# A weight word's masked bits and exponent in one PSUM bank, two banks for attention's small products, and a new slot table

## The chip, the cores and the metric

The kernel runs on one core of a Trainium2 chip. The metric is the device time of one execution in microseconds (us); three runs of the kernel before gave 510.4, 511.69 and 512.15 us, a median of 511.69.

## The reference, cut to what matters

Three layers run one after another: clustered attention, a dense layer with a rational activation, and a soft mixture of experts.

```python
q_assign = argmax(einsum('bhsd,hcd->bhsc', q_n, c_n))      # nearest of 16 centroids
k_assign = argmax(einsum('bhsd,hcd->bhsc', k_n, c_n))
scores = where(q_assign == k_assign, scale * q @ k.T, -1e9)  # 2 batches, 8 heads, 768 x 768
x = softmax(scores) @ v                                     # -> 1536 tokens x 512
h = x @ w_in                                                # 512 x 2048, given as float64
g = (a0 + a1*h + a2*h*h + a3*h**3) / (1 + |b0|*|h| + |b1|*h*h + 1e-6)
x = g @ w_out                                               # 2048 x 512, given as float64
logits = x @ phi; d = softmax(logits, 0); c = softmax(logits, 1)
out = c @ experts(d.T @ x)                                  # 8 experts, 4 slots each
```

The weights `w_in` and `w_out` come as 64-bit floats. The kernel makes 32-bit values of them itself, from the two 32-bit words of each.

## The kernel before, in words

Attention is a list of 96 units (8 pairs of heads, 12 blocks each) that one loop takes through slots n = -2 to 101 (lines 744 to 796). The order on each engine is the order in which this loop emits instructions; nothing is reordered. In slot n PE turns unit n's exponentials around (`turn`, L486, six transposes), multiplies the scores of unit n+2 (`a1_mm`, L460 and L458, four matmuls into a two-bank tile), runs the slot's small products, and some value products (`a2_av`, L499; how many is the digit of `AV`). VectorE runs the slot's small steps and then `a1_neg` of unit n+2 (L471): it reads the scores, writes them negated to SBUF and takes their minimum. ScalarE takes the exponential of unit n+1 (L475), copies unit n's turned block (L492) and runs its small steps. The score tile is a single one; unit 1's scores alone lie in the tile of the turned blocks (line 452).

The small steps are laid out by hand: `SLOT` (line 114) gives the slot of each step, and `RANK` (line 168) its engine group and its place in the slot. The groups are L and S (DMAs on SyncE), D (VectorE), G (GpSimd), A (ScalarE), P and T (PE, ahead of and behind the value products). Some steps prepare the next pair of heads (scores against the centroids, one-hot masks, high and low parts of q and k); some end a group of rows (over, wide, rows, wider, split); and some decode weights.

Decoding (`decode_steps`, line 607) takes 32 pieces of 128 x 512 weights, one SBUF tile of raw words each. `ex` masks the exponent bits of the high word, `mh` its mantissa bits, both from SBUF to SBUF on VectorE (L617). `expo` (ScalarE, L626) shifts and rebases the exponent in place. `mant` (VectorE, L629) adds the low word, scaled, to the masked bits, in place; `sign` (VectorE, L633) puts the sign on the exponent, in place. `value` (GpSimd, L638) multiplies the two. Further steps split or transpose and store the result.

All small products of PE (centroid scores L364, their transposes L374, masks L401, row factors L520, weight transposes L670, products with phi L679, L691) take a bank of the PSUM pool `psM`, three banks (line 104). A bank comes free when the reader of that product, on VectorE or ScalarE, is done. Pair 1's centroid scores are computed at the very start, right after the first scores.

Of the kernel before, what the change touches and what calls it, by code (L numbers as in the profile page):

```python
# [52 lines left out]
def tile_kernel(ctx, tc, qk, v, cenT, cenP, consts, constsb, ab, w_in, w_out, phi, w1, w2, out, dbg=None):  # L53
# [50 lines left out]
    psM = actx.enter_context(tc.tile_pool(name="psM", bufs=3, space=PSUM))  # L104
# [12 lines left out]
        scT=(0, 11, 17, 28, 40, 53, 67),
        best=(1, 12, 18, 29, 42, 55, 68),
        equal=(1, 13, 19, 29, 44, 55, 69),
        rank=(2, 13, 22, 30, 44, 55, 70),  # L120
        least=(3, 14, 23, 31, 45, 56, 70),
        alone=(4, 15, 23, 31, 47, 57, 71),
        turn=(4, 16, 24, 32, 47, 59, 73),
        masks=(5, 17, 26, 34, 48, 61, 74),
        high=(1, 9, 21, 34, 44, 57, 69),
        klow0=(1, 9, 21, 34, 46, 57, 71),
        klow1=(1, 14, 22, 39, 46, 58, 71),
        qlow0=(5, 10, 23, 38, 46, 60, 71),
        qlow1=(6, 15, 26, 38, 50, 62, 71),
        own0=(2, 10, 27, 40, 53, 67, 72),  # L130
        own1=(2, 18, 30, 38, 51, 62, 73),
        cross0=(7, 17, 30, 41, 55, 65, 80),
        cross1=(7, 17, 31, 39, 54, 65, 74),
        low0=(3, 19, 32, 40, 47, 64, 78),
        low1=(3, 15, 28, 41, 55, 64, 77),
        mask0=(6, 19, 32, 42, 53, 66, 78),
        mask1=(6, 20, 31, 42, 55, 66, 78),
        over=(7, 13, 19, 26, 32, 37, 44, 49, 56, 62, 67, 74, 81, 86, 91, 98),
# [16 lines left out]
        value=(3, 7, 8, 11, 14, 16, 20, 21, 25, 26, 29, 34, 37, 38, 40, 43, 45, 48, 50, 55, 56, 59, 63, 66, 68, 72,
               74, 76, 80, 81, 85, 88),
        store=(6, 8, 14, 14, 22, 20, 27, 25, 30, 34, 35, 36, 38, 40, 46, 45, 51, 50, 57, 56, 64, 60, 69, 71, 74,
               74, 82, 78, 87, 83, 91, 90),
        hpart=(4, 8, 18, 23, 28, 30, 37, 40, 48, 52, 61, 66, 72, 74, 83, 88),
# [1278 lines left out]
```

## Time and profile before

| | |
|---|---|
| median of three runs | 511.69 us (510.4 to 512.15) |
| the profiled execution | 510.94 us, span 509.1 us, granted clock 0.995 |
| PE busy | 495.1 us, 97% of the span |
| VectorE (DVE) busy | 403.3 us, 79% |
| ScalarE (ACT) busy | 369.5 us, 73% |
| GpSimd (POOL) busy | 272.7 us, 54% |

A row of a timeline begins with the start and the duration in us, then engine, line, operation, the output and inputs by the program's names, and in square brackets the idle time before it with what ended it. A row by line gives how many instructions there are, and the shortest, the median and the longest in ns. PE's matmuls are pipelined and their ends are modelled, so a gap of PE is drawn somewhat too short. Attention lies between about 15 and 265 us, and the dense layer and the experts behind it.

### The profile page before, as it was taken

Reading aid. Unit: us, or ns where it says so; the run is one execution under the profiler, and the core shown is the slowest. Engines: PE = TensorE matmul, PEld = TensorE weight load, DVE = VectorE, ACT = ScalarE, POOL = GpSimd, SP = SyncE. Lnnn points to the kernel's source line nnn. Section 1 sums busy time; section 2 is a strip of 40 time slices with the busy share of each in tenths; the row PEclk is TensorE's granted clock in tenths of the full one; section 3 lists DMA queues with packets and bytes.
Section 4 is the critical chain, followed back from the end, with each engine's and each line's share of the span. In section 5 each row is a group of like instructions: output and inputs, shape, how many; then the busy total and the mean of one; then the engine's idle time right before and its main releaser. Section 6 shows DMA issues by size and latency. Waiting matters only on the chain.

```text
span 509.1 us, 9715 instructions
## 1 busy us (share of the span) xinstructions
PE 495.1 (97%) x3452; PEld 336.6 (66%) x3454; DVE 403.3 (79%) x748; ACT 369.5 (73%) x653; POOL 272.7 (54%) x305
## 2 busy tenths in 40 slices
PE   7999999999999999899999999999999999999995
PEld 2667576766767566666666877776777767764363
DVE  5797989999998978978643999999799996985022
ACT  5788888888879798797863988888588776871111
POOL 2556497677683876754425755565456544651000
PEclk8999999999999999999999999999999999999999
DMA  7979798898979699882222777675567765799998
GB/s 226 255 218 267 246 271 265 241 296 233 266 225 221 237 260 238 252 216 110 82 86 101 259 268 258 238 241 208 203 224 251 256 223 192 284 339 408 420 416 321
DMA packets 40671, 124.99 MB, mean 245 GB/s; under 512 B 5744, under 2 KB 6896, under 8 KB 36016
## 3 DMA queue, kind: packets, MB, share of 16 engines
q1 hardware_dynamic: 40048, 123.66, 75.5%
q10 hardware_dynamic: 576, 0.72, 0.4%
q8 instruction: 27, 0.44, 0.4%
q14 instruction: 20, 0.16, 0.1%
HBM read 89.56 MB, written 15.73 MB: 207 GB/s over the span
## 4 chain that ended last, share of the span: by engine, by line
PE 76%; DMA 11%; DVE 8%; ACT 2%; issue 1%; ACTq 0%; DVEq 0%; SPq 0%
PE sT L486 11%; PE av L499 11%; PE h L862 9%; PE h L865 9%; PE h L863 9%; DMA wt<-w 7%; PE s L460 6%; PE s L458 5%; PE gt L909 4%; DVE e L471 3%; DMA raw<-w_in 2%; PE l L921 2%; PE dg L983 1%; DMA w_in<-w 1%; DVE mh L629 1%
## 5 line engine op out<-in xcount | busy, mean ns | idle before, releaser
L475 ACT ACTIVATE e<-e,nv 128x768 f32<-128x768 f32 x96 | 90.0, 938 | 36.1 <-DVE e L471 33.8
L471 DVE TENSOR_SCALAR_CACHE_REDUCE e<-s 128x768 f32<-128x768 f32 x96 | 91.6, 954 | 30.2 <-PE s L458 26.0
L486 PEld LDWEIGHTS sT<-cst,e 128*128 128x128 f32 x576 | 61.5, 140 | 44.2 <-ACT eT L492 21.4
L486 PE MATMUL sT<-cst,e 128*128 128x128 f32 x576 | 83.4, 281 | 1.5 <-DVE e L471 0.7
L862 PE MATMUL h<-xh,w 128*128 128x512 f32 x192 | 80.6, 420 | 0.0
L492 ACT COPY eT<-sT 128x768 f32<-128x768 f32 x96 | 75.3, 784 | 4.9 <-PE sT L486 4.6
L863 PE MATMUL h<-xl,w 128*128 128x512 f32 x192 | 75.2, 392 | 0.0
L499 PE MATMUL av<-eT,vt 128*64 128x384 f32 x384 | 75.1, 501 | 0.0
L460 PE MATMUL s<-op 128*128 128x384 f32 x192 | 72.9, 381 | 2.2 <-DVE e L471 1.8
L879 POOL TENSOR_SCALAR q<-u,babs 128x512 f32<-128x512 f32 x47 | 36.4, 775 | 68.8 <-ACT u L877 68.8
L638 POOL TENSOR_TENSOR w<-mh,ex 128x516 f32<-128x516 f32 x32 | 42.1, 1314 | 47.3 <-DVE ex L633 34.9
L458 PE MATMUL s<-op 80*128 80x384 f32 x192 | 64.7, 338 | 0.2 <-ACT op L296 0.2
L881 POOL TENSOR_TENSOR q<-q,u 128x512 f32<-128x512 f32 x47 | 61.0, 1298 | 3.9
L865 PE MATMUL h<-xh,w 128*128 128x512 f32 x192 | 52.9, 396 | 0.0
L877 ACT ACTIVATE u<-h 128x512 f32<-128x512 f32 x47 | 27.9, 594 | 29.0 <-PE h L865 29.0
L862 PEld LDWEIGHTS h<-xh,w 128*128 128x128 f32 x192 | 36.1, 188 | 16.3 <-DVE p L894 5.0
L880 DVE TENSOR_TENSOR p<-p,h 128x512 f32<-128x512 f32 x47 | 32.1, 683 | 15.6 <-ACT p L878 15.5
L865 PEld LDWEIGHTS h<-xh,w 128*128 128x128 f32 x192 | 36.0, 188 | 8.6
L863 PEld LDWEIGHTS h<-xl,w 128*128 128x128 f32 x192 | 36.2, 189 | 6.7 <-issue 0.5
L499 PEld LDWEIGHTS av<-eT,vt 128*64 128x64 f32 x384 | 22.6, 135 | 26.2 <-issue 24.7
L460 PEld LDWEIGHTS s<-op 128*128 128x128 f32 x192 | 36.2, 189 | 4.6 <-DVE e L471 3.8
L887 ACT ACTIVATE r<-q,epsc 128x512 f32<-128x512 f32 x47 | 32.8, 697 | 8.2 <-POOL q L881 6.7
(203 smaller groups left out, 938.3 us busy)
## 6 DMA issues: line engine op xcount, KB each, us to landing
wt<-w SPq DMA_DIRECT2D x32, 1024.0 KB, 7.0
w<-w_in SPq DMA_DIRECT2D x96, 256.0 KB, 3.1
op<-split SPq DMA_DIRECT2D x42, 384.0 KB, 7.1
raw<-w_in SPq DMA_DIRECT2D x16, 512.0 KB, 6.1
raw<-w_out SPq DMA_DIRECT2D x16, 512.0 KB, 5.9
w_in<-w SPq DMA_DIRECT2D x16, 512.0 KB, 5.8
raw<-qk SPq DMA_DIRECT2D x7, 768.0 KB, 7.3
w_out<-w SPq DMA_DIRECT2D x16, 256.0 KB, 4.3
```

The costliest lines, as they stand in the source:

```text
L458: PE.matmul(ps[:, c, 0:HS], o["q2"][rows, it], o["k2"][rows, w], start=False, stop=True)
L460: PE.matmul(ps[:, c, 0:HS], o["q1"][:, it], o["k1"][:, w], start=True, stop=False)
L471: DVE.tensor_scalar(e, s1s.pop(u)[:, :, 0:HS], -(D ** -0.5), None, ALU.mult, ALU.min, accum_out=nvs[g][:, rest:rest + 1])
L475: ACT.activation(es[u], es[u], AF.Exp, scale=-1.0, bias=nvs[g][:, rest:rest + 1], accum_out=sums[g][:, rest:rest + 1])
L486: PE.transpose(ps[:, j // 3, j % 3 * 128:(j % 3 + 1) * 128], e[:, j, :], ident)
L492: ACT.copy(dst, eTp.pop(u)[:, :, 0:HS].rearrange("p c (j t) -> p c j t", j=3))
L499: PE.matmul(av[g][64 * h:64 * h + 64, 0:HS], vs[g // 2][:, h, j, :], eTs[g][:, h, j, :], start=(j == 0), stop=(j == 5))
L638: POOL.tensor_tensor(w.rearrange("p (r n) -> p r n", r=3), hold["mh"].bitcast(F32), hold["ex"].bitcast(F32), ALU.mult)
L862: PE.matmul(h, wh[:, c, :], xh[t][:, c, :], start=(c == 0), stop=False)
L863: PE.matmul(h, wh[:, c, :], xl[t][:, c, :], start=False, stop=False)
L865: PE.matmul(h, wl[:, c, :], xh[t][:, c, :], start=False, stop=(c == NCC - 1))
L881: POOL.tensor_tensor(q, q, u, ALU.mult)
```

## The change

The raw tile becomes 4 x 128 words in place of 3 x 172, so that all operations take 512 elements and no pad has to be cleared. A pool `psD` of one PSUM bank is new, and `psM` has two banks in place of three. `mh` writes the masked mantissa bits to the bank of `psD`; `mant` reads them there, with the low word from SBUF, and writes to an SBUF tile of its own. After that `expo` reads the exponent bits in SBUF and writes the exponent to the same bank; `sign` reads it there, with the high word from SBUF, and writes to the SBUF tile of `ex`. `value` reads SBUF as before. Pair 1's centroid scores take the bank of `psD` too. `SLOT` and the digits of `AV` are new throughout; of the table the diff below keeps the lines of the decode steps (the first few pieces) and of a few more, and `RANK` stays.

```diff
-    psM = actx.enter_context(tc.tile_pool(name="psM", bufs=3, space=PSUM))
+    psM = actx.enter_context(tc.tile_pool(name="psM", bufs=2, space=PSUM))
+    psD = actx.enter_context(tc.tile_pool(name="psD", bufs=1, space=PSUM))
...
-        scaled=(-1, 10, 16, 27, 39, 51, 65),
+        scaled=(-1, 10, 15, 30, 40, 53, 65),
...
-        ex=(0, 2, 5, 9, 11, 14, 15, 17, 22, 23, 26, 30, 33, 36, 38, 40, 41, 44, 49, 50, 54, 57, 58, 61, 64, 67, 70,
+        ex=(-1, 4, 5, 9, 12, 14, 18, 21, 23, 27, 29, 31, 33, 36, 39, 41, 45, 47, 48, 51, 52, 55, 61, 62, 64, 67,
...
-        mh=(-1, 5, 7, 9, 11, 13, 16, 17, 21, 25, 27, 29, 32, 35, 38, 39, 42, 44, 48, 49, 52, 57, 59, 60, 65, 69,
+        mh=(-1, 3, 6, 8, 11, 15, 17, 20, 23, 25, 28, 31, 33, 35, 38, 41, 44, 46, 49, 51, 53, 58, 60, 62, 65, 67,
...
-        expo=(1, 2, 6, 9, 12, 14, 15, 17, 22, 24, 28, 31, 33, 36, 38, 41, 44, 45, 49, 52, 55, 58, 61, 62, 66, 68,
+        expo=(1, 5, 7, 10, 13, 16, 18, 21, 24, 27, 29, 32, 34, 36, 39, 42, 45, 48, 50, 52, 54, 59, 61, 63, 66, 68,
...
-        mant=(2, 6, 8, 10, 13, 16, 18, 21, 25, 26, 28, 32, 34, 37, 39, 41, 43, 46, 49, 51, 53, 59, 61, 62, 66, 71,
+        mant=(0, 5, 7, 9, 13, 16, 18, 21, 24, 26, 29, 32, 34, 36, 39, 42, 45, 48, 50, 52, 54, 59, 61, 63, 66, 68,
...
-        sign=(3, 6, 7, 11, 14, 15, 17, 20, 24, 25, 29, 33, 34, 37, 40, 43, 45, 47, 50, 53, 56, 59, 62, 63, 67, 69,
+        sign=(2, 6, 8, 11, 14, 17, 20, 22, 25, 28, 30, 33, 35, 37, 40, 43, 46, 49, 51, 53, 56, 60, 62, 65, 67, 69,
...
-            m = hold["m"] = m_tile()
+            m = hold["m"] = psD.tile([128, 512], F32, tag="d", name="d") if p == 1 else m_tile()
...
-    raw64 = [dec_p.tile([128, 3, 172, 2], I32, name=f"raw64{i}") for i in range(NRAW)]
-    for t in raw64:
-        POOL.memset(t.rearrange("p r n t -> p (r n t)")[:, 1024:1032], 0)
+    raw64 = [dec_p.tile([128, 4, 128, 2], I32, name=f"raw64{i}") for i in range(NRAW)]
...
-        def bits(n, *of):
-            hold[n] = dec_p.tile([128, 3, 173], I32, tag=n, name=n, bufs=2)[:, :, 0:172]
-            DVE.tensor_scalar(hold[n], raw[:, :, :, 1], *of)
+        def words_(n):
+            return dec_p.tile([128, 4, 129], I32, tag=n, name=n, bufs=2)[:, :, 0:128]
+
+        def bank():
+            return psD.tile([128, 512], F32, tag="d", name="d").bitcast(I32).rearrange("p (r n) -> p r n", r=4)
...
         def mh():
-            bits("mh", 0xfffff, 0x100000, ALU.bitwise_and, ALU.bitwise_or)
+            hold["high"] = bank()
+            DVE.tensor_scalar(hold["high"], raw[:, :, :, 1], 0xfffff, 0x100000, ALU.bitwise_and, ALU.bitwise_or)
+
+        def mant():
+            hold["mh"] = words_("mh")
+            DVE.scalar_tensor_tensor(hold["mh"].bitcast(F32), raw.bitcast(U32)[:, :, :, 0], 2.0 ** -32,
+                                     hold.pop("high"), ALU.mult, ALU.add)
 
         def expo():
-            ACT.activation(hold["ex"], hold["ex"], AF.Relu, bias=epsc[:, 2:3], scale=8.0)
-
-        def mant():
-            DVE.scalar_tensor_tensor(hold["mh"].bitcast(F32), raw.bitcast(U32)[:, :, :, 0], 2.0 ** -32, hold["mh"],
-                                     ALU.mult, ALU.add)
+            hold["power"] = bank()
+            ACT.activation(hold["power"], hold["ex"], AF.Relu, bias=epsc[:, 2:3], scale=8.0)
 
         def sign():
-            DVE.scalar_tensor_tensor(hold["ex"], raw[:, :, :, 1], -2 ** 31, hold["ex"],
+            DVE.scalar_tensor_tensor(hold["ex"], raw[:, :, :, 1], -2 ** 31, hold.pop("power"),
                                      ALU.bitwise_and, ALU.bitwise_or)
...
     AV = [int(c) for c in
-          "211020110220201120210003120120"
+          "301110201021102102021030103101"
```

## Rows read from the trace of the kernel before

**Rows 1.** Ten stretches: length, then busy us of PE, PEld, DVE, ACT, POOL (instructions); clock, DMA.

```profile
18.00:30.00 12.00, 10.76 (x68) 7.52 (x69) 10.27 (x21) 9.26 (x17) 4.27 (x5) 1.00 1.05 249
...
55.00:62.00 7.00, 6.59 (x42) 3.87 (x40) 7.00 (x14) 5.88 (x10) 2.67 (x3) 1.00 0.64 171
...
203.00:209.00 6.00, 4.73 (x34) 2.93 (x32) 6.00 (x10) 3.75 (x8) 5.84 (x7) 1.00 0.79 200
...
sum 247.00, PE 243.56 PEld 165.50 DVE 211.37 ACT 206.01 POOL 155.06; mean PE 24.36 PEld 16.55 DVE 21.14 ACT 20.60 POOL 15.51
```

**Rows 2.** Waits of PE, 18 to 270 us: us in total, times, longest.

```profile
PE s L460 <- DVE e L471: 1.8, 4, 0.8
PE sT L486 <- DVE e L471: 0.7, 1, 0.7
```

**Rows 3.** Chain that ended last, two stretches (50-62, 200-210 us): start us, us, what.

```profile
52.65 1.22 DVE mh L629
...
58.28 1.50 DVE ex L633
...
204.30 1.08 DVE eq L394
...
205.40 1.49 DVE mh L629
```

**Rows 4.** Groups of VectorE by line, 16 to 270 us: busy us, mean ns, idle before.

```profile
L471 DVE TENSOR_SCALAR_CACHE_REDUCE e<-s 128x768 f32<-128x768 f32 x96 | 91.6, 954 | 30.2 <-PE s L458 26.0 <-ACT eT L492 2.5 <-ACT e L475 0.9
L629 DVE SCALAR_TENSOR_TENSOR mh<-raw,mh 128x516 f32<-128x516 uint32 x32 | 26.9, 842 | 0.0
L633 DVE SCALAR_TENSOR_TENSOR ex<-raw,ex 128x516 int32<-128x516 int32 x32 | 26.9, 840 | 0.9 <-ACT ex L626 0.8
...
L471 DVE DVE_READ_ACCUMULATOR e<-s 128x1 f32 x96 | 7.9, 82 | 0.0
```

**Rows 5.** Mantissa and sign steps by line: ns min/median/max, first and last start.

```profile
L629 DVE SCALAR_TENSOR_TENSOR mh<-raw,mh x32: 652/698/1494, 23.9 to 242.8; 128x516 f32<-128x516 uint32 x32
...
L633 DVE SCALAR_TENSOR_TENSOR ex<-raw,ex x32: 681/694/1501, 27.3 to 245.3; 128x516 int32<-128x516 int32 x32
```

**Rows 6.** Second-stage instructions of VectorE with an operand in PSUM, by line.

```profile
L882 DVE SCALAR_TENSOR_TENSOR p<-p,ncoef,h x47: 736/741/748, 271.2 to 446.7; 128x512 f32<-128x512 f32 x47
...
L895 DVE SCALAR_TENSOR_TENSOR r<-q,epsc,r x46: 748/750/755, 279.0 to 446.0; 128x512 f32<-128x512 f32 x46
```

**Rows 7.** Costliest groups of the page: busy us, mean ns, idle before.

```profile
L475 ACT ACTIVATE e<-e,nv 128x768 f32<-128x768 f32 x96 | 90.0, 938 | 36.1 <-DVE e L471 33.8
...
L486 PE MATMUL sT<-cst,e 128*128 128x128 f32 x576 | 83.4, 281 | 1.5 <-DVE e L471 0.7
...
L492 ACT COPY eT<-sT 128x768 f32<-128x768 f32 x96 | 75.3, 784 | 4.9 <-PE sT L486 4.6
...
L881 POOL TENSOR_TENSOR q<-q,u 128x512 f32<-128x512 f32 x47 | 61.0, 1298 | 3.9
```

**Rows 8.** ScalarE's exponent step, and an activation into PSUM, by line.

```profile
L626 ACT ACTIVATE ex<-ex,epsc x32: 721/727/739, 22.5 to 244.5; 128x516 int32<-128x516 int32 x32
...
L887 ACT ACTIVATE r<-q,epsc x47: 687/692/715, 275.8 to 446.6; 128x512 f32<-128x512 f32 x47
```

**Rows 9.** Instructions in order of time, 15 to 20 us: start us, us, what.

```profile
16.57 0.70 DVE L617 TENSOR_SCALAR mh<-raw 128x516 int32<-128x516 int32 x1
...
17.18 0.94 DVE L471 TENSOR_SCALAR_CACHE_REDUCE e<-s 128x768 f32<-128x768 f32 x1
...
17.75 0.58 ACT L369 ACTIVATE sc<-mf,pc 128x384 f32<-128x384 f32 x1
...
18.29 0.85 PE L486 MATMUL sT<-cst,e 128*128 128x128 f32 x6 [0.66 <-DVE e L471]
```

**Rows 10.** The same, 24 to 27 us.

```profile
24.54 0.70 DVE L617 TENSOR_SCALAR ex<-raw 128x516 int32<-128x516 int32 x1
...
26.29 0.45 PE L460 MATMUL s<-op 128*128 128x384 f32 x1 [0.55 <-DVE e L471]
```

More of the change, by code (lines that the diff above doesn't have):

```diff
@@ L114, in tile_kernel @@
     SLOT = dict(
-        scores=(-2, 9, 14, 26, 38, 50, 63),
-        scaled=(-1, 10, 16, 27, 39, 51, 65),
[L117 to L138, printed above, removed]
@@ L155, in tile_kernel @@
[L155 to L159, printed above, removed]
-        lpart=(4, 12, 18, 23, 28, 31, 37, 41, 48, 55, 61, 67, 72, 78, 84, 89),
-        flip=(9, 12, 19, 23, 28, 35, 42, 45, 51, 55, 62, 69, 74, 77, 82, 88),
@@ L162, in tile_kernel @@
-        tkeep=(10, 13, 20, 25, 30, 36, 43, 46, 53, 57, 64, 72, 75, 78, 85, 89),
-        phi=(11, 17, 23, 26, 32, 37, 44, 47, 54, 59, 71, 74, 77, 79, 86, 89),
-        keep=(13, 19, 24, 27, 35, 38, 45, 48, 55, 62, 73, 75, 82, 85, 87, 90),
-        fin=(27, 48, 79, 91),
-        summed=(28, 49, 81, 92),
+        scores=(-2, 9, 14, 29, 39, 52, 63),
+        scaled=(-1, 10, 15, 30, 40, 53, 65),
+        scT=(0, 11, 18, 31, 42, 54, 66),
+        best=(1, 12, 19, 32, 43, 56, 68),
+        equal=(1, 13, 19, 32, 43, 56, 68),
@@ new lines, in tile_kernel @@
+        rank=(2, 13, 19, 33, 43, 57, 69),
+        least=(3, 15, 22, 34, 44, 57, 69),
+        alone=(4, 15, 23, 37, 47, 58, 74),
+        turn=(4, 15, 24, 37, 48, 58, 74),
+        masks=(5, 17, 25, 38, 49, 60, 75),
+        high=(1, 9, 21, 33, 45, 57, 69),
+        klow0=(1, 10, 24, 35, 46, 58, 69),
+        klow1=(1, 10, 25, 36, 46, 59, 69),
+        qlow0=(5, 10, 25, 35, 50, 60, 69),
+        qlow1=(6, 13, 26, 38, 50, 61, 74),
+        own0=(2, 18, 29, 39, 53, 67, 76),
+        own1=(2, 15, 24, 41, 53, 68, 72),
@@ new lines, in tile_kernel @@
+        cross0=(7, 18, 27, 43, 56, 67, 75),
+        cross1=(7, 18, 27, 42, 52, 63, 76),
+        low0=(3, 18, 30, 39, 56, 61, 74),
+        low1=(3, 14, 26, 39, 48, 65, 79),
+        mask0=(6, 20, 29, 43, 54, 68, 79),
+        mask1=(6, 20, 32, 41, 53, 65, 78),
+        over=(7, 15, 19, 25, 31, 37, 43, 49, 55, 61, 67, 74, 79, 85, 92, 97),
+        wide=(7, 15, 19, 26, 33, 38, 45, 49, 56, 62, 68, 74, 79, 85, 93, 97),
+        rows=(7, 16, 22, 27, 34, 39, 46, 50, 58, 64, 69, 74, 80, 86, 93, 98),
@@ new lines, in tile_kernel @@
+        wider=(8, 17, 23, 29, 35, 41, 47, 51, 59, 65, 70, 75, 81, 87, 94, 99),
+        split=(17, 18, 26, 32, 39, 43, 53, 54, 61, 68, 72, 79, 89, 95, 99, 101),
+        words=(-2, 0, 2, 5, 8, 11, 14, 17, 19, 22, 26, 29, 31, 35, 38, 40, 42, 43, 44, 48, 51, 53, 59, 61, 62, 66,
+               69, 72, 74, 75, 79, 80),
+        ex=(-1, 4, 5, 9, 12, 14, 18, 21, 23, 27, 29, 31, 33, 36, 39, 41, 45, 47, 48, 51, 52, 55, 61, 62, 64, 67,
+               71, 73, 76, 80, 82, 84),
+        mh=(-1, 3, 6, 8, 11, 15, 17, 20, 23, 25, 28, 31, 33, 35, 38, 41, 44, 46, 49, 51, 53, 58, 60, 62, 65, 67,
+               70, 73, 76, 79, 81, 83),
@@ L167, in tile_kernel @@
+        keep=(12, 20, 24, 27, 34, 39, 44, 47, 56, 63, 64, 69, 81, 84, 90, 91),
+        fin=(27, 48, 70, 91),
+        summed=(28, 50, 71, 92),
     )
@@ L619, in ex @@
         def ex():
-            bits("ex", 0x7ff00000, None, ALU.bitwise_and)
+            hold["ex"] = words_("ex")
+            DVE.tensor_scalar(hold["ex"], raw[:, :, :, 1], 0x7ff00000, None, ALU.bitwise_and)
         def mh():
-            bits("mh", 0xfffff, 0x100000, ALU.bitwise_and, ALU.bitwise_or)
+            hold["high"] = bank()
[4 more added lines that the diff above has]
+                                     hold.pop("high"), ALU.mult, ALU.add)
```

36 lines of the change are left out of this document (18 added, 18 removed).

## The prediction, made before the changed kernel was run

> **What bounds the kernel now.** I read the busy shares first: PE has work nearly all the time, so the first question is in which stretches it does not. The table of stretches [rows 1] answers it for attention: of the 247 us from 18 to 265 us, PE is busy 243.56, idle 3.44. That idle time is lumpy: 1.25 us in 18 to 30 us, 0.41 in 55 to 62 and 1.27 in 203 to 209. After 265 us nothing that the change touches runs, and the end follows attention's end one to one.
>
> The waits of PE in the same stretch [rows 2] name who ends these gaps: the negated-score instruction of VectorE (L471), 1.8 us in 4 waits, and 0.7 at the start. The matrix unit waits, because a score bank can't be refilled before L471 has read it, and L471 stands in VectorE's queue behind that slot's small steps. The chain that ended last, in 50 to 62 us [rows 3], shows which: a mantissa step of 1.22 us and a sign step of 1.50 us. In 200 to 210 us it passes a rank product (L394) of 1.08 us and a mantissa step of 1.49. A matmul's end is modelled (576 transposes are drawn 281 ns long and fill 83.4 us, 145 ns each [rows 7]), so some 0.15 to 0.25 us of each gap is hidden. With seven or so gaps after 30 us I put the true idle time there at 2.2 us (3.44 less 1.25) plus about 1.6, or 3.8 us. That is the most that any relief of VectorE can give behind the start.
>
> The costliest VectorE groups [rows 4] show the burden: L471 954 ns once a slot and its accumulator read 82 ns, mantissa (L629) 842 and sign (L633) 840 ns, 32 times each. The spread of those two [rows 5] is the point: medians of 698 and 694 ns, longest 1494 and 1501. So most of them take 0.69 us and some twice that.
>
> **The change part by part.** *One operand of mantissa and sign comes from PSUM.* The nearest rows are the three-operand VectorE instructions of the second stage that read one tensor from SBUF and one from PSUM [rows 6]: 736 to 748 ns in 47, 748 to 755 in 46, for 512 elements and with a scalar taken from a tensor. None of them is long, though GpSimd's two-input products run for 61.0 us beside them [rows 7]. So I take the long cases as gone. Uncontended price: between 0.69 us (the median of today's form, four elements more) and 0.745 (the middle of the two second-stage forms); I take 0.70, since the scalar here is a constant as in today's form. Saved: 64 x (0.841 - 0.70) = 9.0 us of VectorE time, bounds 64 x 0.096 = 6.1 and 64 x 0.151 = 9.7.
>
> [...]
>
> *The masked high bits and the exponent are written to PSUM.* No row shows VectorE's tensor-scalar from SBUF to PSUM; a three-operand instruction that writes PSUM takes 750 ns where its like that writes SBUF takes 741 [rows 6], so 0 to +0.01 us, times 32: nothing. ScalarE's exponent step takes a median of 727 ns for 516 elements; a ScalarE activation from SBUF to PSUM takes 692 for 512 [rows 8]. That is 32 x 0.035 = 1.1 us of ScalarE time, bounds 0 and 1.1; its cover, if it is a loss, is that ScalarE's exponential waits 36.1 us in all, mostly for L471 [rows 7].
>
> *512 instead of 516 elements, and three tiny memsets less:* under 1%, on GpSimd and VectorE; nothing at the end.
>
> *What 9 us of VectorE time is worth.* A slot of attention lasts 247/96 = 2.57 us on PE, and L471 with its read takes 1.04, so 1.53 us is left for the small steps of a slot. There are 13 kinds of these; the view of rows 4 has the mean of each, and its first two stand there. Adding them up slot by slot in the old table, 42 of 96 slots go over that, by 18.7 us in all; with the new table and the two steps at 0.69, 33 slots by 13.0 us (14.5 at 0.745). Most of that excess is caught by slots that PE fills with more value products; only the clusters stall. The new table still has slots of 2.4 to 2.6 us (33, 43, 15). With a quarter to a third of the overload gone and the longest single delays (1.2 and 1.5 us) gone altogether I expect half of the 3.8 us: -1.9 us, bounds 0 and -3.8.
>
> *psM with two banks.* By the two tables, a small product takes a bank that ScalarE gave back one slot earlier 27 times instead of 11, and one that VectorE gave back in the same slot 12 times instead of 5 (of 72). ScalarE's step of slot n-1 stands before its next exponential, and PE's small products of slot n stand behind six transposes (0.85 us in rows 9) and four score matmuls. So the bank is mostly free by then. Cost: 0 to +0.6 us, I take 0.1.
>
> *A new wait at the start.* Pair 1's centroid scores now go to the new bank, and word 0's masked bits (mh0), in slot -1, want the same bank. They can't be written before ScalarE's scaled step has read the scores. In the rows of the start [rows 9], mh runs at 16.57 between the first two L471, and the scaled step runs from 17.75 to 18.33. In the changed kernel mh0 waits for 18.33 and something for the signal, and what is queued behind it on VectorE is the second L471: it starts at about 18.4 + 0.61 = 19.0 instead of 17.18. The first transposes wait for that L471 already (0.66 us at 18.29), since unit 1's scores lie in their bank. So all of attention starts about 1.85 us later. Part returns: the ex step that makes the score matmul of 26.29 late (0.70 us at 24.54, then 0.55 us of waiting [rows 10]) leaves slot 2 for slots -1 and 4. I take 1.85 - 0.70 = +1.15 us; bounds +0.5 (if slack of later slots takes more) and +1.9.
>
> *One bank for a word's whole chain.* mh, mant, expo, sign, one word after another. Three of the hand-overs stay on VectorE's own queue or come a slot later; ScalarE's expo, which was free to run before mant, now waits for mant of its own slot. ScalarE's exponential and copy of that slot come first and take 0.94 and 0.78 us [rows 7], so mant is done. sign now comes one slot after expo in 28 of 32 words, in 20 before; that wait cost 0.8 us in all [rows 4]. I take +0.05 at the end; the rival below has its other bound.
>
> *DMA and SyncE:* the same bytes and counts; the words' loads have as many slots of lead or more. Nothing.
>
> **The sum.** -1.9 + 0.1 + 1.15 + 0.05 = -0.6 us, against the profiled execution's 510.94 us (span 509.1, the rest lies around it): 510.3. That execution is 0.75 us under the median of the three runs, 511.69; a median of the changed kernel should come at 511.69 - 0.6 = 511.1 us. A measurement of this kernel tells about 0.3% (1.5 us) from no change, so this is no change that can be told.
>
> **The rivals.** (1) *Faster: the contention was all of it.* The rare long cases make the clusters, without them the table holds, and the 3.8 us go; with the start's +1.15 this gives 509.0, with a start that is absorbed 507.9. For it: the long steps in the chain, one of them just before the worst gap [rows 3]. Against: the rank product over two SBUF tensors there (L394), which the change leaves as it is.
> (2) *Slower: the one bank ties VectorE to ScalarE.* In a slot ScalarE's exponential (0.94), copy (0.78), sometimes a step like the scaled one (0.58) and expo (0.70) end 2.4 to 3.0 us after L471's end; sign may start one slot, 2.57 us, after the same point. From where expo's end comes later than the next L471's end, VectorE stands at sign, and the slot's ex, mh and L471 stand behind it. If half of the 28 pay 0.3 us, that is 4.2 us, about half of it seen by PE (+2.1); with the start at +1.85 and half of the relief lost (-0.95), +3.0: 514.7. Against: 20 words stood at one slot before, and all of them waited 0.8 us together.
> (3) *The change doesn't do what it says:* mantissa and sign stay at 0.84 us. Then only the start counts, +1.15 to +1.9: 513.2. Against it are rows 6 and 7.
>
> **How the numbers follow.** Forecast 0.45, rival 1 0.32, rival 2 0.18, rival 3 0.05. Rival 3 lies half in the band of 0.3%. Faster 0.32, within 0.47, slower 0.21. The range reaches to rival 1 and half way into rival 2: 508.3 to 513.8.
>
> **What would show it.** In the changed kernel's trace: mantissa and sign all at 0.68 to 0.75 us, none over 0.8; VectorE 8 to 10 us less busy in attention; the second L471 at about 19 us and the first transposes at about 20; gaps of PE between 50 and 210 us half as large; waits of sign for expo under 2 us in all. The prediction is wrong if the first transposes still start at 18.3, if PE's idle time behind 30 us goes to nothing or grows, or if PE waits for ScalarE's releases of the two small banks.

## The result, and the profile after

The changed kernel takes 514.12 us in the median (511.76 to 518.34), beside 510.93 for the kernel before (508.47 to 513.66). The ratio is 1.007, with a 95% interval of 1.005 to 1.009: slower by 0.7%, some 3.5 us. The forecast was 511.1 us and its range ended at 513.8. Ratios are of runs taken beside each other and not the quotient of two medians, from which they differ by up to 0.3%; two runs of e4, over 1.5% above its fastest one, are left out of its numbers. The profiled execution took 516.06 us (span 514.3). In the code after, the lines of attention stand one lower: L471 is L472 there, L486 is L487; `ex` is L622, `mh` L626, `mant` L630, `sign` L638.

What the change was made to do, it does. By line and shape, VectorE from 15 to 280 us (busy us, mean ns, then the idle time before, with what ended it):

```profile
L472 DVE TENSOR_SCALAR_CACHE_REDUCE e<-s 128x768 f32<-128x768 f32 x96 | 91.7, 955 | 43.0 <-PE s L459 31.9 <-ACT eT L493 7.5 <-ACT e L476 3.0
L626 DVE TENSOR_SCALAR d<-raw 128x512 int32<-128x512 int32 x32 | 22.1, 690 | 1.0 <-ACT sc L370 0.5
L638 DVE SCALAR_TENSOR_TENSOR ex<-raw,d 128x512 int32<-128x512 int32 x32 | 21.8, 681 | 1.4 <-ACT d L635 1.0
L630 DVE SCALAR_TENSOR_TENSOR mh<-raw,d 128x512 f32<-128x512 uint32 x32 | 21.7, 679 | 0.0
L622 DVE TENSOR_SCALAR ex<-raw 128x512 int32<-128x512 int32 x32 | 19.8, 618 | 0.8 <-DMA raw<-w_in 0.8
```

Mantissa and sign took 842 and 840 ns [rows 4]; they take 679 and 681. By line, with the shortest, the median and the longest of each in ns:

```profile
L630 DVE SCALAR_TENSOR_TENSOR mh<-raw,d x32: 647/680/708, 18.5 to 243.9; 128x512 f32<-128x512 uint32 x32
...
L638 DVE SCALAR_TENSOR_TENSOR ex<-raw,d x32: 646/680/708, 27.3 to 247.1; 128x512 int32<-128x512 int32 x32
...
L622 DVE TENSOR_SCALAR ex<-raw x32: 385/430/1505, 16.1 to 242.2; 128x512 int32<-128x512 int32 x32
```

None of the two is over 708 ns, though an instruction of GpSimd runs beside 41 of the 64; before, the longest were 1494 and 1501 [rows 5], all 24 over 750 ns had one beside them, and the 21 that had none took 0.68 to 0.70 us. That is 10.3 us less of VectorE in 64 steps. `ex` has changed unforeseen: its median is 430 ns, where a mask took 0.70 us before [rows 9, 10], but its longest is 1505. The page's busy row:

```profile
PE 497.7 (97%) x3452; PEld 338.7 (66%) x3454; DVE 392.2 (76%) x748; ACT 369.3 (72%) x653; POOL 262.1 (51%) x302
```

VectorE is down by 11.1 us from 403.3. PE is up by 2.6 us from 495.1, though it has the same 3452 instructions. Where that lies is seen at the start; the instructions of the three engines in order of time (start, duration, and in brackets the idle time before with its releaser):

```profile
16.07 0.43 DVE L622 TENSOR_SCALAR ex<-raw 128x512 int32<-128x512 int32 x1 [0.80 <-DMA raw<-w_in]
...
16.38 0.58 ACT L370 ACTIVATE sc<-d,pc 128x384 f32<-128x384 f32 x1
...
17.00 0.69 DVE L626 TENSOR_SCALAR d<-raw 128x512 int32<-128x512 int32 x1 [0.50 <-ACT sc L370]
17.60 0.95 DVE L472 TENSOR_SCALAR_CACHE_REDUCE e<-s 128x768 f32<-128x768 f32 x1
...
18.70 1.51 PE L487 MATMUL sT<-cst,e 128*128 128x128 f32 x6 [2.45 <-DVE e L472]
```

mh (L626) waits for ScalarE's scaled step, the second L472 is behind it, and the first transposes start at 18.70 us behind 2.45 us of idle time. They then take 1.51 us, where they took 0.85 [rows 9]. The stretches show at which clock (columns as in rows 1; the granted clock is the third number from the end):

```profile
18.00:20.00 2.00, 1.30 (x7) 1.33 (x7) 1.16 (x3) 1.03 (x2) 1.92 (x3) 0.56 1.06 345
20.00:25.00 5.00, 5.00 (x25) 4.16 (x23) 2.08 (x4) 2.75 (x5) 0.27 (x1) 0.50 1.05 250
25.00:30.00 5.00, 4.82 (x28) 3.25 (x29) 4.55 (x10) 3.25 (x7) 1.96 (x2) 0.99 1.02 286
```

TensorE's granted clock was 0.56 in 18 to 20 us and 0.50 in 20 to 25 us, and 0.99 behind that; in the kernel before, 18 to 30 us had 1.00 throughout [rows 1]. The waits of PE, 18 to 270 us:

```profile
PE sT L487 <- DVE e L472: 2.4, 1, 2.4
PE s L461 <- DVE e L472: 1.5, 2, 1.2
PE sT L487 <- ACT eT L493: 0.6, 2, 0.4
```

Behind the start, its waits for L472 come to 1.5 us in 2 cases, 1.2 the longest; they were 1.8 in 4 [rows 2]. For 50 to 210 us in one piece, after and then before:

```profile
50.00:210.00 160.00, 158.01 (x1114) 107.07 (x1113) 137.14 (x276) 132.90 (x236) 103.99 (x122) 1.00 0.95 251
```

```profile
50.00:210.00 160.00, 157.99 (x1098) 106.47 (x1097) 145.55 (x272) 134.50 (x237) 111.68 (x122) 1.00 0.90 248
```

PE's idle time there was 160 - 157.99 = 2.01 us and is 1.99. VectorE has 8.4 us less to do in it, and PE got nothing for that. From 30 to 265 us PE's idle time even grew, from 2.2 to 2.6 us, which is one of the prediction's own signs of being wrong. The largest gap after:

```profile
102.77 1.50 DVE L622 TENSOR_SCALAR ex<-raw 128x512 int32<-128x512 int32 x1
...
104.19 0.68 DVE L626 TENSOR_SCALAR d<-raw 128x512 int32<-128x512 int32 x1
...
104.79 0.94 DVE L472 TENSOR_SCALAR_CACHE_REDUCE e<-s 128x768 f32<-128x768 f32 x1
...
105.79 0.44 PE L461 MATMUL s<-op 128*128 128x384 f32 x1 [1.17 <-DVE e L472]
```

Here one `ex` of 1.50 us, not a mantissa or a sign, delays mh and L472, and PE stands idle for 1.17 us.

### The profile page after: what moved, and what is told of

Same layout as the page of the kernel before. It is cut to its first block, busy times and chain, and to the rows that moved or that the text cites. A ratio compares the mean times of both kernels' runs of the same rounds, so it can differ in the third digit from the quotient of the medians.

```text
span 514.3 us, 9728 instructions
## 1 busy us (share of the span) xinstructions
PE 497.7 (97%) x3452; PEld 338.7 (66%) x3454; DVE 392.2 (76%) x748; ACT 369.3 (72%) x653; POOL 262.1 (51%) x302
## 4 chain that ended last, share of the span: by engine, by line
PE 75%; DMA 9%; DVE 7%; ACT 3%; POOL 3%; issue 2%; SPq 0%; ACTq 0%; POOLq 0%; DVEq 0%
PE av L500 11%; PE sT L487 11%; PE h L866 9%; PE h L869 8%; PE h L867 8%; PE s L461 5%; PE s L459 5%; DMA wt<-w 4%; PE gt L913 3%; PE pf L1278 3%; PE l L925 2%; DVE e L472 2%; DMA w_out<-w 2%; DMA op<-split 1%; PE dg L987 1%
## 5 line engine op out<-in xcount | busy, mean ns | idle before, releaser
L472 DVE TENSOR_SCALAR_CACHE_REDUCE e<-s 128x768 f32<-128x768 f32 x96 | 91.7, 955 | 43.0 <-PE s L459 31.9
L487 PEld LDWEIGHTS sT<-cst,e 128*128 128x128 f32 x576 | 63.0, 142 | 41.6 <-ACT eT L493 17.3
L487 PE MATMUL sT<-cst,e 128*128 128x128 f32 x576 | 84.3, 283 | 3.3 <-DVE e L472 2.4
L643 POOL TENSOR_TENSOR w<-mh,ex 128x512 f32<-128x512 f32 x32 | 42.2, 1319 | 40.1 <-DVE ex L638 34.1
```

The source lines that it names most:

```text
L472: DVE.tensor_scalar(e, s1s.pop(u)[:, :, 0:HS], -(D ** -0.5), None, ALU.mult, ALU.min, accum_out=nvs[g][:, rest:rest + 1])
L487: PE.transpose(ps[:, j // 3, j % 3 * 128:(j % 3 + 1) * 128], e[:, j, :], ident)
L643: POOL.tensor_tensor(hold["w"].rearrange("p (r n) -> p r n", r=4), hold["mh"].bitcast(F32), hold["ex"].bitcast(F32), ALU.mult)
```

## The experiments

Theory A: the shared bank at the start costs the 0.7%, by the wait and by the lower clock behind it. Theory B: the new form of `ex`, fast but contending with GpSimd (in the changed kernel 0.41 to 0.43 us in the 8 steps with no instruction of GpSimd beside them, up to 1.50 in the 24 with one), took the gain of the interior. Theory C: the new table, or the missing bank, did. Every ratio is to the kernel before, run beside it.

### The start

**e1: pair 1's scores back in a psM bank.**

```diff
-            m = hold["m"] = psD.tile([128, 512], F32, tag="d", name="d") if p == 1 else m_tile()
+            m = hold["m"] = m_tile()
```

> The changed kernel, but pair 1's centroid scores take a bank of psM again, so that nothing at the start waits for the new bank. [...] Theory B (the interior: the ex step now runs in a form that contends with GpSimd): no change but the 1.2 us that I had given to the wait, 512.5 to 514.1.

Measured: 511.27 us, ratio 1.0001 [0.9979, 1.0022]. This one line carries the whole loss: 1.0070 less 1.0001 is 0.69%, 3.5 us (2 to 5 by the two intervals). In order of time:

```profile
16.40 0.43 DVE L622 TENSOR_SCALAR ex<-raw 128x512 int32<-128x512 int32 x1 [1.06 <-DMA raw<-w_in]
16.44 0.58 ACT L370 ACTIVATE sc<-mf,pc 128x384 f32<-128x384 f32 x1
16.74 0.69 DVE L626 TENSOR_SCALAR d<-raw 128x512 int32<-128x512 int32 x1
...
17.34 0.95 DVE L472 TENSOR_SCALAR_CACHE_REDUCE e<-s 128x768 f32<-128x768 f32 x1
...
18.44 0.84 PE L487 MATMUL sT<-cst,e 128*128 128x128 f32 x6 [2.13 <-DVE e L472]
```

The wait for the bank is gone, but mh comes only 0.26 us earlier, since `ex` ahead of it waits for the word's own DMA. The transposes start 0.26 us earlier too, with 2.13 us of idle time before them. But the stretches show the clock at 1.00:

```profile
18.00:20.00 2.00, 1.56 (x14) 1.35 (x16) 0.90 (x3) 1.67 (x3) 1.92 (x3) 1.00 1.05 349
20.00:25.00 5.00, 4.90 (x34) 3.35 (x35) 4.67 (x10) 4.06 (x8) 0.63 (x2) 1.00 1.02 220
```

Unit 3's L472 ends at 23.19 us here and at 26.26 in the changed kernel. So of 3.07 us in the two profiles, 0.26 is the later start and 2.8 comes behind it, at the lower clock. Not every run is like these two. Over all runs the mean granted clock is 0.9913 after and 0.9952 here (0.9956 to 0.9965 in the runs of before, group by group). Half the clock for T us takes 0.5 T / 512 from the mean, so the changed kernel spends 0.0039 x 512 / 0.5 = 4.0 us more at the lower level in the mean run. If PE were at work through all of it, half would be lost: 2.0 us, an estimate from the clocks, and a high one. The mean counts idle stretches as well (in the changed kernel's profile PE is done at 509.4 us, and the clock is 0.50 from 510 to the end), and between runs of one kernel 0.001 of the mean clock goes with 0.27 us, not with 0.51 (348 runs of 20 kernels): by that the clock's part is about 1.0 us. What is left of the 3.5 us, 1.5 to 2.5, would be the wait itself, but that is a remainder and not shown: the profiles have the start only 0.26 us later than here, and 0.9 in e5 below.

**e2: the changed kernel, with idle matmuls on PE while it waits.**

```diff
             a1_mm(1)
             nxt()
+            idle(11)
```

> The changed kernel with 11 more filler matmuls (0.216 us each, 2.4 us) on TensorE between pair 1's scores and the first transposes, where it waited 2.45 us. The wait itself stays. [...] Theory A2 (the wait alone is the cost): no change within 0.5 us, 513.6 to 514.6.

Measured: 512.52 us, ratio 1.0035 [1.0013, 1.0057], mean clock 0.9968. In order of time, and then the stretches:

```profile
16.36 2.32 PE L570 MATMUL rest<-zero 128*128 128x512 bf16 x10 [0.16 <-issue]
...
16.94 0.69 DVE L627 TENSOR_SCALAR d<-raw 128x512 int32<-128x512 int32 x1 [1.05 <-ACT sc L371]
...
18.64 0.84 PE L488 MATMUL sT<-cst,e 128*128 128x128 f32 x6
```

```profile
18.00:20.00 2.00, 2.00 (x14) 1.36 (x11) 1.10 (x3) 1.47 (x3) 1.90 (x2) 1.00 1.00 310
20.00:25.00 5.00, 4.90 (x36) 3.43 (x35) 4.56 (x10) 4.10 (x8) 0.00 (x0) 1.00 1.02 237
```

The wait for the scaled step is as long as ever, and the first transposes start no earlier. Yet half of the loss is gone, and the clock is at 1.00. With the higher estimate from e1 this agrees: about half of the 0.7% was the clock. The intervals allow anything from a tenth to nearly all of it, and e6 and e13 below say how far e2 can be read.

**e3: the kernel before with the wait, a first try that missed.**

```diff
+        late = plan[n].pop("D") if n == -1 else []
         run(n, ("S", "D", "G"))
...
         run(n, "A")
+        if late:
+            DVE.tensor_copy(s2_p.tile([128, 1], F32, tag="gate", name="gate"), scs[0][:, 0:1])
+        for step in late:
+            step[-1]()
```

> The kernel before, with the start wait of the changed kernel alone: VectorE's mh of word 0 stands behind a one-column copy that reads the result of ScalarE's scaled step of pair 1, and the second L471 behind both. Theory A: the first transposes come 1.8 us later; with the lower clock that may follow, +2 to +3.5 us on the kernel before (513 to 514.4). Theory B: at most the 1.2 us of the prediction (511 to 512.1).

Here `late` is word 0's mh, and `scs` (lines not shown) collects the tiles that the scaled steps write. Measured: 510.94 us, ratio 0.9997 [0.9978, 1.0017]. `scs[0]` is the tile of pair 0, which is written earlier, so the copy waited for nothing, as its row shows:

```profile
14.91 0.15 DVE L787 COPY gate<-sc 128x1 f32<-128x1 f32 x1
...
15.88 0.69 DVE L620 TENSOR_SCALAR mh<-raw 128x516 int32<-128x516 int32 x1 [0.81 <-DMA raw<-w_in]
...
17.58 0.84 PE L489 MATMUL sT<-cst,e 128*128 128x128 f32 x6 [1.60 <-DVE e L474]
```

It can be read as another execution of the kernel before, and as the control of e5. mh waits for the word itself, 0.81 us. The transposes start at 17.58 us, not at 18.29 [rows 9]; yet that is 1.50 us behind the scaled step's start at 16.08, where [rows 9] have 0.54: the start differs by as much from one execution to the next.

**e5: the same with the tile of pair 1.** `scs[0]` became `scs[1]`.

> The kernel before, with one wait added at its start: word 0's masked bits (mh0) come after a one-column copy on VectorE of the scaled tile of pair 1, so they wait until ScalarE has scaled pair 1's scores, as in the changed kernel. Table, decode in SBUF and three banks stay. (The first try at this, e3, copied the tile of pair 0, which is written earlier, and added no wait.) Theory A, the start's wait, with the lower granted clock that follows it, is what costs the 0.7%: the first transposes start at 18.5 to 19 us behind some 2 us of idle time instead of 18.29, the granted clock is half for some microseconds behind 18 us, unit 3's L471 ends 1.5 to 3.5 us later than before, and the whole takes 512.3 to 514.4 us (ratio 1.003 to 1.007). Theory B, the new decode, two banks and table cost it: ratio 0.999 to 1.002.

Measured: 513.20 us, ratio 1.0053 [1.0029, 1.0078], mean clock 0.9921. In order of time, then the stretches:

```profile
16.72 0.15 DVE L787 COPY gate<-sc 128x1 f32<-128x1 f32 x1 [1.72 <-ACT sc L372]
16.80 0.69 DVE L620 TENSOR_SCALAR mh<-raw 128x516 int32<-128x516 int32 x1
...
18.51 0.85 PE L489 MATMUL sT<-cst,e 128*128 128x128 f32 x6 [2.53 <-DVE e L474]
```

```profile
18.00:20.00 2.00, 1.49 (x9) 1.52 (x10) 0.97 (x3) 1.60 (x3) 1.92 (x3) 0.85 1.07 314
20.00:25.00 5.00, 5.00 (x31) 3.88 (x31) 3.31 (x7) 2.84 (x6) 0.08 (x1) 0.72 1.01 204
```

With nothing else of the change, the wait makes three quarters of the loss, with the clock that follows it: 2.53 us of idle time, transposes 0.9 us later than in e3, the clock down. This and e1 are one edit from both sides, and agree with theory A.

**e6: e5 with the `idle(11)` of e2; e13: the kernel before with that `idle(11)` alone.**

> As e5, and PE runs eleven idle matmuls behind the second unit's scores, so that it is not idle while it waits. Theory A with the clock as the larger part: the granted clock stays at 1.0 behind 18 us, and only the wait itself is left: ratio 1.000 to 1.002 (510.8 to 511.9), below e5 by 1 to 2.5 us. Theory A with the wait alone as the larger part: as e5, ratio 1.003 to 1.006.

> The kernel before with the eleven idle matmuls of e2 and e6 at the start, and no wait. If they cost nothing: ratio 0.998 to 1.001, and e6's 0.59% is the added wait's own. If they cost something with the old table: ratio 1.002 to 1.005, and the wait's own price in e6 is the rest, 0.1 to 0.4%.

Measured: e6 513.18 us, ratio 1.0059 [1.0036, 1.0083], clock 0.9969; e13 513.04 us, 1.0047 [1.0031, 1.0063], clock 0.9961. The clock is back up in e6, and the time is that of e5 all the same: taken alone, that speaks against the clock. But the idle matmuls themselves cost 0.47% with the old table (e13). A part of that is their own length; e13, in order of time:

```profile
16.48 0.95 DVE L472 TENSOR_SCALAR_CACHE_REDUCE e<-s 128x768 f32<-128x768 f32 x1
...
18.44 0.82 PE L487 MATMUL sT<-cst,e 128*128 128x128 f32 x6
```

The second L472 is done at 17.4 us, but PE works on the idle matmuls from 16.28 on, and the transposes start at 18.44, some 0.9 us later than they could. In e6 they start at 18.78. So the 0.12% from e13 to e6 (-0.2 to +0.4%) prices a later start by 0.3 us and not the whole wait, and how much of e5's loss is the clock these runs do not settle. Nor do they say why the idle matmuls cost 2.4 us in e13 and nothing in e12 below, where they hold the transposes back by about as much: the profiled execution of e13 was the fastest of its runs (511.43 us).

### The interior

**e4: the changed kernel, with `ex` in the 3 x 172 form; e11: e1 with the same.**

```diff
-            DVE.tensor_scalar(hold["ex"], raw[:, :, :, 1], 0x7ff00000, None, ALU.bitwise_and)
+            DVE.tensor_scalar(t[:, :, 0:172], rawp[i % NRAW][:, :, :, 1], 0x7ff00000, None, ALU.bitwise_and)
```

> The changed kernel with the ex step alone in the old shape (3 rows of 172 words out of a padded raw tile, into rows 173 apart). What follows reads the first 512 words of that tile, so that the weights are left with other values; every instruction and wait stays. Theory B (ex in the even shape is a fast form, 0.42 us, that waits for GpSimd or makes it wait, up to 1.5 us): ex takes 0.68 us in all 32, none over 0.75, the gaps of TensorE at 57, 105 and 148 us go, and the time falls by 1 to 2.5 us against the changed kernel (511.6 to 513.1). Theory A: no change (513.6 to 514.6), or slower, since VectorE has 32 x 0.06 us more to do.

> The changed kernel with pair 1's scores back in a psM bank (as e1) and its ex step reading and writing in the 3 x 172 form of before (as e4; its elements land elsewhere, so the output is not the reference's). In that form ex should take 0.68 us each time and not 0.42 to 1.5. Theory, ex's contention with GpSimd took part of the interior's gain: ratio to before 0.995 to 0.998, below e1 by 1 to 2.5 us. Rival, the mean of 0.62 against 0.68 us makes both the same: ratio 0.999 to 1.002.

Measured: e4 514.1 us in ten runs, ratio 1.0037 [1.0004, 1.007]; e11 511.18 us, 1.001 [0.9989, 1.003]. The edit took hold (e11, VectorE by line):

```profile
L629 DVE TENSOR_SCALAR ex<-raw 128x516 int32<-128x516 int32 x32 | 21.9, 684 | 1.1 <-DMA raw<-w_in 0.8 <-DMA raw<-w_out 0.2
```

The mean is 684 ns, where the fast form had 618, and the long cases are gone (650 to 716 ns in e11). On e1 it brings nothing, and e4's interval reaches from no change to that of the changed kernel. Theory B falls as a cause of the 0.7%, though the gap at 105 us is real.

**e8: the ceiling.** The kernel before, mantissa and sign on 24 of 512 elements:

```diff
-            DVE.scalar_tensor_tensor(hold["ex"], raw[:, :, :, 1], -2 ** 31, hold["ex"],
+            DVE.scalar_tensor_tensor(hold["ex"][:, :, 0:8], raw[:, :, 0:8, 1], -2 ** 31, hold["ex"][:, :, 0:8],
```

> The kernel before, with the mantissa and sign steps on 24 of 512 elements each (the rest of the weights keeps its masked bits, so the output is not the reference's): VectorE loses some 40 us of small steps in attention, four times what the change can bring. This is the ceiling for any relief of those steps. As predicted (half of 3.8 us for 9 us of relief): PE's waits for L471 behind 30 us nearly vanish, 3 to 4 us less, ratio 0.992 to 0.994 (507 to 508). Rival, PE's gaps in the interior are worth much less than drawn, since what one slot loses a later one had spare: ratio 0.997 to 1.000 (509.3 to 510.9), with the gaps gone from the trace or moved to other waits.

Measured: 507.19 us, ratio 0.9931 [0.9906, 0.9956]: 3.5 us. The steps went to 304 and 295 ns in the mean, 35 us of VectorE in all, and the waits of PE, 18 to 270 us, are all but gone:

```profile
PE sT L486 <- DVE e L471: 0.5, 1, 0.5
PE s L460 <- DVE e L471: 0.3, 1, 0.3
```

So 3.8 us as the most that relief of VectorE can give was sound (2.2 to 4.8 by the interval). But it took 35 us to get it, not 9.

**e9: the relief alone, with the old table.** GpSimd's product on 24 of 512 elements:

```diff
-            POOL.tensor_tensor(w.rearrange("p (r n) -> p r n", r=3), ...
+            POOL.tensor_tensor(w.rearrange("p (r n) -> p r n", r=3)[:, :, 0:8], ...
```

> The kernel before, with GpSimd's product of mantissa and exponent on 24 of 512 elements (the rest of the weights is zero, so the output is not the reference's): table, banks and VectorE's own instructions are untouched, and GpSimd no longer runs beside mantissa and sign for long. It is what the prediction wanted of the change, without the rest of the change. If the relief is worth what was predicted with the old table: mantissa and sign under 0.75 us in the mean, ratio 0.994 to 0.997 (507.4 to 509). Rival, the old table had the contention laid where it costs nothing: same durations, ratio 0.998 to 1.001.

Measured: 509.99 us, ratio 0.9982 [0.9964, 1.0001]: 0.9 us, up to 1.8. VectorE by line:

```profile
L637 DVE SCALAR_TENSOR_TENSOR ex<-raw,ex 128x516 int32<-128x516 int32 x32 | 25.5, 796 | 1.1 <-ACT ex L630 1.0
L633 DVE SCALAR_TENSOR_TENSOR mh<-raw,mh 128x516 f32<-128x516 uint32 x32 | 25.2, 789 | 0.0
```

Only about a third of the excess over 0.69 us went (842 and 840 to 789 and 796). In the kernel before, 20 of the 24 mantissa and sign steps over 0.75 us have other steps of GpSimd beside them and not this product. So it says that some relief of 3 us is worth something near 1 us, and no more than that.

**e7: the new table alone; e10: the same with mantissa and sign as in e8.** The edit is the `SLOT` and `AV` of the change, in the kernel before; e10 has e8's diff besides.

> The kernel before with the new slot table and new digits for the value products alone: decode from SBUF to SBUF in the 3x172 form, three banks, pair 1's scores in one of the three. Mantissa and sign then still contend with GpSimd (means 0.82 to 0.85 us). Theory C, the new table is worse in itself and took the gain of the two cured steps: ratio 1.003 to 1.006 (512.3 to 514). Rival, the table is neutral and only tuned to the start: ratio 0.998 to 1.002. If the table in itself is better: under 0.997.

> The new table and digits in the kernel before (as e7), with mantissa and sign on 24 of 512 elements each (as e8; the rest of the weights keeps its masked bits, so the output is not the reference's). e7 lost 1.26% by the table, and its mantissa steps took 957 ns in the mean instead of 842. Theory, the table is bad only with contending steps: with these gone it is as good as e8, ratio 0.991 to 0.996. Rival, the table costs something besides (ScalarE's steps, PE's products, the start): ratio 0.998 to 1.006, that is 2.5 to 6 us above e8.

Measured: e7 517.39 us, ratio 1.0126 [1.0093, 1.0159]; e10 510.31 us, 0.9979 [0.9956, 1.0001]. In e7, VectorE by line:

```profile
L629 DVE SCALAR_TENSOR_TENSOR mh<-raw,mh 128x516 f32<-128x516 uint32 x32 | 30.6, 957 | 0.0
L633 DVE SCALAR_TENSOR_TENSOR ex<-raw,ex 128x516 int32<-128x516 int32 x32 | 27.3, 854 | 0.8 <-ACT ex L626 0.7
```

Mantissa went up from 842 to 957 ns, and its longest step from 1494 to 1715. That the new table lays more of these steps beside GpSimd was the author's estimate and is not shown. The table came with steps that take 0.65 to 0.71 us beside GpSimd or not, and with those of before it is poor. From e7 to e1, which cures them (and has two banks), the time falls by 1.25%. With the steps short in both tables, e10 is 0.48% above e8, about 2.5 us (3.1 by the medians; 0.8 to 4.1 by the intervals). A part of that is the start; PE's waits in e10:

```profile
PE sT L486 <- DVE e L471: 2.0, 1, 2.0
PE s L460 <- DVE e L471: 0.2, 1, 0.2
```

There is a wait of 2.0 us before the first transposes, which was 0.5 in e8: the new table has ex as well as mh of word 0 between the first two L471. In the interior PE waits no more than in e8. What the rest is, the trace doesn't name. It is the price with short steps; that it is the same with those of the change isn't shown.

**e14: e10 with two psM banks; e15 and e16: e8 with a part of the new table.**

```diff
-    psM = actx.enter_context(tc.tile_pool(name="psM", bufs=3, space=PSUM))
+    psM = actx.enter_context(tc.tile_pool(name="psM", bufs=2, space=PSUM))
```

For e15 the rows `words` to `keep` of `SLOT` are the new ones, for e16 `scores` to `mask1`.

> e10 (new table, mantissa and sign on 24 of 512 elements each, so the output is not the reference's) with two banks for attention's small products in place of three. The prediction put the lost bank at 0.1 us, 0 to 0.6. As predicted: as e10, ratio 0.997 to 0.999 to before. Rival, two banks hold PE up more than that: 1 to 3 us above e10, ratio 1.000 to 1.004, with waits of PE for ScalarE's or VectorE's readers of small products.

> e8 (the kernel before, mantissa and sign on 24 of 512 elements each, so the output is not the reference's) with the new table's rows for the decode steps (words to keep) alone; the other rows and the digits of the value products are the old ones. If the decode rows carry the table's cost (ex and mh both in slot -1, expo and mant in one slot): ratio 0.996 to 0.999, near e10. If not: 0.992 to 0.994, as e8.

> e8 (as in e15) with the new table's rows for the steps that prepare the next pair of heads (scores to mask1) alone. If these carry the table's cost: ratio 0.996 to 0.999, near e10. If not: 0.992 to 0.994, as e8. If both e15 and e16 are as e8, the digits and the rows that end a group carry it.

Measured: e14 510.85 us, ratio 1.0007 [0.998, 1.0035]; e15 523.81 us, 1.0263 [1.0227, 1.0299]; e16 518.82 us, 1.0161 [1.013, 1.0191]. e14 is 0.28% above e10 with intervals that overlap: two banks cost between nothing and some 3 us, and its profile shows no wait for a bank. e15 and e16 are misses: half a table is far worse than either whole one, so a table can't be split into the part that costs.

### The versions that might beat both

**e12: e1 with the `idle(11)` of e2. e17: e1, with nothing of the decode between the first two L471. e18: the same in the kernel before.**

```diff
-        ex=(-1, 4, 5, 9,
+        ex=(0, 4, 5, 9,
-        mh=(-1, 3, 6, 8,
+        mh=(0, 3, 6, 8,
-        mant=(0, 5, 7, 9,
+        mant=(1, 5, 7, 9,
```

In e18 only mh of word 0 moves, from -1 to 0.

> The changed kernel with pair 1's scores in a psM bank (as e1) and eleven idle matmuls on PE behind the second unit's scores (as e2). In e1 the clock stayed at 1.0 behind 18 us without them, in e2 with them. If the clock at the start costs in some runs of e1 too: 0.5 to 1.5 us below e1, ratio 0.997 to 0.999. If not: as e1, ratio 0.999 to 1.001. This is also the candidate for a kernel that is better than both.

> The changed kernel with pair 1's scores in a psM bank (as e1), and word 0's mh and ex in slot 0 and its mant in slot 1, so that nothing of the decode stands between the first two L471. In e1 mh0 waited 1.06 us there for the word itself. If that stretch sets the start: first transposes at 16.5 to 17.3 us instead of 18.44 and no long idle time before them, ratio to before 0.996 to 0.999 (1 to 2 us below e1). Rival, slots 0 and 1 are then too full for VectorE and give it back: as e1, ratio 0.999 to 1.002.

> The kernel before with word 0's mh in slot 0 in place of -1; all else as before. If the stretch between the first two L471 sets the start: first transposes at 16.5 to 17.3 us instead of 18.29, ratio 0.997 to 0.999. Rival, slot 0 gives it back: ratio 0.999 to 1.002.

Measured: e12 511.11 us, ratio 1.0015 [0.9991, 1.0038]; e17 509.37 us, 0.9992 [0.9974, 1.0009]; e18 509.62 us, 1.0000 [0.9981, 1.0019]. The first transposes, in e17 and in e18:

```profile
16.39 0.84 PE L487 MATMUL sT<-cst,e 128*128 128x128 f32 x6 [0.37 <-DVE e L472]
```

```profile
16.53 0.85 PE L486 MATMUL sT<-cst,e 128*128 128x128 f32 x6 [0.37 <-DVE e L471]
```

They start 1.8 to 2.1 us earlier than before [rows 9] and in e1, with 0.37 us of idle time, and e17's mean clock is 0.9972. The execution of [rows 9] was late as a whole, though. Counted from the start of the scaled step the transposes come after 0.23 us in e17 and 0.24 in e18, after 0.54 in [rows 9], 1.50 in e3 and 2.00 in e1. By the intervals that is worth between nothing and about 2 us from e1 to e17, and at most 1 us either way from the kernel before to e18. e17 recovers what the changed kernel lost, and none of the versions is shown to beat the kernel before.

## Why the prediction was wrong

**Mantissa and sign: right.** All at 0.65 to 0.71 us, none over 0.8, 10.3 us saved where 9.0 stood. The 0.745 us of [rows 6] was too high: the row of today's form was the nearer one. The median is 680 ns with the PSUM operand and was 698 and 694 without, for 512 elements and 516. VectorE's 8 to 10 us less came as 8.4 in 50 to 210 us and 11.1 over the span.

**Where the miss lies.** The sum said -0.6 us, and the change cost 3.5. Two steps failed. The wait at the start, 1.85 us before anything returned, came as 3.5: 1.65 of the miss. The rest of the sum, -1.9 + 0.1 + 0.05 and the 0.70 that was to return, -2.45 in all, came as 0.0 (e1, which has all of it but the wait): 2.45 of the miss. The base of 511.69 us, the median of three runs, was also 0.76 above that of fifteen.

**The start: right in place, mis-sized.** "So all of attention starts about 1.85 us later" became 3.5 us (e1 against the result, 2 to 5 by the intervals; 2.7 in e5, 1.5 to 4.0). How much of that is the later start itself is not settled: 1.5 to 2.5 us as the remainder in e1, 0.3 and 0.9 by the profiles of e1 and of e3 and e5. What has no term in the sum is the granted clock. The idle time that the wait leaves on PE, 2.4 us in one piece, is followed by a lower clock in most runs (13 of 15 have a mean under 0.995, and with idle matmuls in that place 1 of 12 in e2), and what follows is then done more slowly (six transposes in 1.51 us for 0.85): for 5 + 2 x 0.44 / 0.5 = 6.8 us in the changed kernel's rows, for 3.4 us in those of e5 by the same sum. The stretches [rows 1] carried the clock column, at 1.00, and the prediction did not ask whether it would stay there behind 2 us of idle time. In 20 to 25 us it is 0.50 in the changed kernel, behind 2.45 us of it, and 0.72 in e5, behind 2.53; in e1, behind 2.13, it is 1.00.

The due times, "about 19" for the second L471 and "about 20" for the transposes, against 17.60 and 18.70, were right but for the start of that one execution. There the clock was already low ahead of attention, and the scaled step stood at 17.75 us [rows 9]; it stands at 16.1 to 16.4 in the profiles after, of e1 and of e5. In the kernel before:

```profile
10.00:14.00 4.00, 4.00 (x21) 1.81 (x19) 2.57 (x5) 1.90 (x4) 1.72 (x4) 0.75 0.89 265
```

Counted from the start of the scaled step the transposes were forecast some 2.3 us behind it, and they are at 2.32. What the late execution hid is word 0: there mh ran without waiting for it, while VectorE waits for its DMA for 0.7 to 1.1 us in the changed kernel, e1, e3 and e13. So in such executions the transposes would not have come, without the new wait, 0.54 us behind the scaled step, as in [rows 9], but 1.5 to 2.0 (e3, e1), and the wait moves them by 0.3 to 0.9 us and not by 1.85.

**The interior: -1.9 did not come.** Without the start's wait the change is worth 0.0% [-0.21, +0.22] (e1). The 0.70 us of [rows 10] did return: from the end of unit 3's L472 to that of unit 4's it is 2.57 us, and was 3.20. Two terms failed. First, what relief is worth: the ceiling of 3.8 us was right (3.5 in e8), but "half of the 3.8 us" for 9 us was generous. e8 paid 35 us of VectorE for 3.5, one tenth, by which 10.3 us bring about 1.0; e9 stands nearer to a third, with an interval that has both, and nothing too. Second, the table: 33 slots over by 13.0 us against 42 by 18.7 made it a help, and it is a price of about 2.5 us (e10 against e8), of which a wait at the start is a part. How these add up to e1's 0.0 is open: -1.0 and +2.5 give +1.5, and the intervals cover the difference. Adding up VectorE's work slot by slot does not tell the worth of a table; e15 and e16, mixes of two tables, lost 1.6 to 2.6%.

**ex in its new shape: not in the sum at all** ("512 instead of 516 elements ... nothing at the end"). It became faster by 0.25 us where nothing runs on GpSimd (0.42 us, from 0.68), and up to 0.8 us slower where something does (1.50). e11 shows that this does not decide the time.

**psM with two banks, +0.1:** not refuted, and not shown (e14). **The bank chain, +0.05:** right. sign waits for expo 1.0 us in all, 0.8 before; rival 2 got the sign of the result, by a mechanism that was not there. Rival 1 is refuted by e1, which has the decode of the changed kernel, with no mantissa or sign over 708 ns there, and gains nothing; rival 3 by the rows of L630 and L638.

What stays open: how the start's 3.5 us divide between the wait and the clock; what of the new table's price is its start, its two banks, and the rest; and what the idle matmuls cost in e13 beside their length.

## What to carry to other kernels

A wait that leaves the matrix unit idle in one piece can cost more than the length forecast for it: here 3.5 us (2 to 5) came for 1.85, with the granted clock at 0.50 in 20 to 25 us behind 2.45 us of idle time, though what share of it is the clock's is open. Price a new wait with the clock column of the stretch, and let nothing that can come later stand ahead of the unit's first operands. A schedule laid out by hand belongs to the durations that it was laid out for: change it alone and change the durations alone before adding up their worth. And relief of an engine that is not the bound is worth what its overloaded places get of it, here a tenth in e8 and perhaps a third in e9.

## What the runs showed of the hardware that was not expected

The same mask over the same words takes 0.65 to 0.70 us in the 3 x 172 form, in all 64 steps of the kernel before, 51 of them beside an instruction of GpSimd. In the 4 x 128 form, from SBUF to SBUF, it takes 0.41 to 0.43 us in the 8 steps with no instruction of GpSimd beside them, and 0.39 to 1.50 us in the 24 with one. mh, with the same input and its output in PSUM, takes 0.67 to 0.70 us in all 32, 28 of them beside GpSimd. Why the new form is fast alone and long beside GpSimd is not shown: from the one form to the other, input and output change together in every run here. What the rows show is that the form of the kernel before had no long masks, also beside GpSimd, and that the change, which took mantissa and sign out of the long cases (0.65 to 0.71 us), put `ex` in.

The granted clock differs from run to run at equal work: in e1 it stayed at 1.00 behind 2.13 us of idle time in the profiled execution, in e11 it was 0.70 in 20 to 25 us behind 2.14, and of e1's 12 runs 8 have a mean over 0.9945; of the changed kernel's 15 only 2 have.
